# One visit of TensorE per chunk: the next chunk's attention products and this chunk's output products in one planned step

## The chip, the cores and the metric

The kernel runs on one core of a Trainium2 chip. The metric is the device time of one execution in microseconds (us). A profile of one execution gives times of single instructions; its span runs from the first to the last instruction.

## What is computed

A state-space layer on 4 sequences of 768 positions with 8 heads (head size 32, state size 16) feeds a two-layer network with 2048 hidden units. Cut to what matters:

```
# per head, chunk by chunk, cum = running sum of log(a)
L  = exp(cum[i] - cum[j]) for i >= j, else 0
M  = (C B^T) * L
y  = M x + (C state) * exp(cum)
state = exp(sum(log a)) * state + sum_j B[j] x[j] exp(cum[-1] - cum[j])
# then, with y laid out as 3072 tokens of 256 values
h  = y @ w_in            # 256 -> 2048
out = (h - tanh(h)) @ w_out   # 2048 -> 256
```

The kernel may choose its own chunk length; the result is the same.

## The kernel before, in words

**Attention.** A sequence is cut into 7 chunks: six of 112 positions and a last one of 96, so there are 28 chunks (0 to 27) in all. The 16 rows of the carried state stand in front of a chunk's 112 rows of x, so that one product over 128 rows gives both terms of y. For a chunk from number 3 on, `chunk_a` (L439) plans four steps. TensorE computes into the PSUM tile `att`, which has one buffer, the differences cum[i] - cum[j] (4 matmuls in bf16, L452) and C B^T (8 matmuls in float32, each run as two passes, L458: 16 records). These work on 9 or 16 rows in each of the array's four bands of rows. ScalarE takes the exponential into the tile `lt` (L462), VectorE multiplies by C B^T (L466), GpSimd clears what lies above the diagonal (L469). `chunk_y` (L478) plans the rest: TensorE computes y = x^T lt (8 float32 matmuls, 16 records, L494) and, unless the chunk is the last of its sequence, the state products b^T x (8 float32 matmuls, 16 records, L502), both into the PSUM tile `y` with one buffer. These use all 128 rows and 32 or 16 columns of the array each. ScalarE copies the state into the next chunk's x (four copies, L507) and writes the upper part of y (`xh`, L514); VectorE writes the rest (`xl`, L519). So y of a chunk waits for the state of the chunk before and for its own `lt`.

**Network.** The 3072 tokens are 12 tiles of 256. The hidden layer is cut into 8 blocks of 256 units; a step is one block of one tile: `mm1` (L530) makes 12 matmuls of 256 columns into the PSUM tile `ph` (two buffers, L545), `act` (L551) computes h - tanh(h) and splits it into two parts `gh` and `gl` on ScalarE and VectorE (L559, L563, L567, L574), and `mm2` (L582), two steps later, makes 12 more matmuls into the tile `po` (in the profile `o`, L595). 12 such matmuls are called a block below. The first four tiles are worked in four sweeps over two hidden blocks each, while the weights arrive and are converted (`conv`, L287); the tiles 4 to 11 follow one after the other. A tile needs y of the two or three chunks that cover its positions.

**What sets the order.** All steps are recorded with an engine, an estimated cost, and the names that they read and write (`Order.__call__`, L73). A planner then fixes the order of the instructions on every engine: `schedule` (L118) is a list scheduler, `plan` (L173) runs it 16 times with priorities from a backward run and random jitter, and 1500 more times with random changes to the priorities of the steps that start in the first 110 units, and keeps the best. Each try draws one random number for each recorded step, from a fixed seed. A step's instructions are then issued in that order as one piece, so nothing of another step comes between them on its engine.

**When chunks are recorded.** At the end of the main function (L812 to L821) each chunk from 3 on has two places among the network's steps: at the first, `chunk_a` is recorded, at the second, one network step later, `chunk_y`. Chunks 10 and 11 belong to tile 4, the first after the sweeps, and are recorded during the sweeps. TensorE's two steps of a chunk, "att" and "y", are separate; the planner may put network blocks between them, and has to leave time between them for the exponential, the product and the mask.

**Loads.** `group` (L360) loads a pair of chunks: four DMAs for B and C (L247), one for x (L259), one for B by rows (L268). Three such groups have buffers. After an odd chunk's y the group three ahead is loaded.

Of the kernel before, what the change touches and what calls it, by code (L numbers as in the profile page):

```python
# [10 lines left out]
F32 = mybir.dt.float32  # L11
# [9 lines left out]
P = 128  # L21
NB, H, S, D, N = 4, 8, 768, 32, 16
# [10 lines left out]
CPG = 2  # L33
# [14 lines left out]
class Order:  # L48
# [12 lines left out]
    def slot(self, tag, bufs):  # L61
        k = self.count[tag] = self.count.get(tag, -1) + 1
        self.fresh[f"{tag}#{k}"] = tag, f"{tag}#{k - bufs}"
        return f"{tag}#{k}"
# [8 lines left out]
    def __call__(self, eng, cost, fn, r=(), w=(), dma=0, after=()):  # L73
        i = len(self.ops)
        hard = {self.writer[n] for n in r if n in self.writer} | set(after)
        soft, chain = set(), set()
        for n in w:
            hard |= self.readers.pop(n, set())
            if n in self.writer:
                j = self.writer[n]  # L80
                if dma and self.ops[j][0] == "DMA":
                    chain.add(j)
                    hard |= self.before[n]
                else:
                    hard.add(j)
            self.writer[n] = i
            whole = self.whole.get(n, n)
            if whole in self.fresh:
                tag, old = self.fresh.pop(whole)
                for o in (old, *self.parts.get(old, ())):  # L90
                    self.dead.add(o)
                    hard |= self.readers.pop(o, set())
                    if o in self.writer:
                        hard.add(self.writer[o])
                if tag in self.taken:
                    soft.add(self.taken[tag])
                self.taken[tag] = self.made[whole] = i
            elif whole in self.made:
                soft.add(self.made[whole])
        for n in (*r, *w):  # L100
            assert n not in self.dead and n not in self.fresh and n in self.writer, n
        for n in r:
            self.readers.setdefault(n, set()).add(i)
        deps = {j: self.lag(self.ops[j][0], eng) if j in hard else 0.0 for j in (hard | soft) - {i}}
        self.ops.append((eng, cost, fn, deps))
        if dma:

            self.ops.append(("DMA", max(0.25, dma / self.RATE), None, {i: 1.4, **{j: 0.0 for j in chain}}))
            for n in r:
                self.readers[n].add(i + 1)  # L110
            for n in w:
                self.writer[n], self.before[n] = i + 1, hard - {i}
        return i
# [94 lines left out]
def tile_ssm_moe(ctx: ExitStack, tc: tile.TileContext, a, x, bn, bc, wts, out):  # L208
    nc = tc.nc
# [147 lines left out]
    def qlen(ck):  # L357
        return QL if ck % CPB == CPB - 1 else Q
# [7 lines left out]
    def operands(ck):  # L366
        d, c = grp[ck // CPG], ck % CPG
        bb = d["bc"][:, :, c * P : (c + 1) * P]
        cc = d["bc"][:, :, CPG * P + c * Q : CPG * P + (c + 1) * Q]
        return bb, cc  # L370
# [66 lines left out]
            chunk_y(ck)  # L437

    def chunk_a(ck):  # L439

        d, k, q = grp[ck // CPG], chs[ck], qlen(ck)
        n_l = k["n_l"] = [slot("lt", NL)]
        n_a = k["n_a"] = slot("att", 1)

        def fn_p():
            at_ = ps_a.tile([P, 4, 4 * P], F32, tag="att", name=f"att{ck}")
            at_ = k["a"] = at_[:, :, 0 : 4 * q].rearrange("p i (k q) -> p i k q", k=4)
            for i in range(4):  # L450
                r = slice(32 * i, 32 * i + 9)
                nc.tensor.matmul(out=at_[:, i, 0:2, :], lhsT=lt_c[r, ck], rhs=rt_c[r, :, ck, N : N + q],  # L452
                                 start=True, stop=True)
            bb, cc = operands(ck)
            for w in range(2):
                for i in range(4):
                    r = slice(32 * i, 32 * i + N)
                    nc.tensor.matmul(out=at_[:, i, 2 + w, :], lhsT=bb[r, w], rhs=cc[r, w, 0:q], start=True, stop=True)  # L458

        def fn_e():  # L460
            k["l"] = p3.tile([P, H, Q], F32, tag="lt", name=f"lt{ck}", bufs=NL)
            nc.scalar.activation(k["l"][:, :, 0:q].rearrange("p (i w) q -> p i w q", i=4), k["a"][:, :, 0:2, :], AF.Exp)  # L462

        def fn_m():
            lt = k["l"][:, :, 0:q].rearrange("p (i w) q -> p i w q", i=4)
            nc.vector.tensor_tensor(out=lt, in0=k["a"][:, :, 2:4, :], in1=lt, op=ALU.mult)  # L466

        def fn_s():
            nc.gpsimd.affine_select(out=k["l"][:, :, 0:q], in_=k["l"][:, :, 0:q], pattern=[[0, H], [1, q]],  # L469
                                    compare_op=ALU.is_ge, fill=0.0, base=N, channel_multiplier=-1)  # L470

        s = ck >= SPAN[0].stop
        op("PE", 0.65, fn_p, r=[d["n_bc"], l_c[s], r_c[s]], w=[n_a])
        op("ACT", 0.92, fn_e, r=[n_a], w=n_l)
        op("DVE", 1.08, fn_m, r=[n_a], w=n_l)
        op("POOL", 1.4, fn_s, w=n_l)

    def chunk_y(ck):  # L478

        d, k, q = grp[ck // CPG], chs[ck], qlen(ck)  # L480
        b, c = divmod(ck, CPB)
        cg = ck % CPG
        n_y = slot("y", 1)
        last = c == CPB - 1
        if c == 0:
            seq[b]["n_xh"] = op.pieces(slot("xh", 2), CPB)
            seq[b]["n_xl"] = op.pieces(slot("xl", 2), CPB)
        n_xh, n_xl = seq[b]["n_xh"][c], seq[b]["n_xl"][c]

        def fn():  # L490
            y = k["y"] = ps_y.tile([P, 2 * H * D], F32, tag="y", name=f"y{ck}")
            for hg in range(2):
                for h in range(4):
                    nc.tensor.matmul(out=y[D * h : D * h + D, hg * Q : hg * Q + q],  # L494
                                     lhsT=d["x"][:, cg, P * hg + D * h : P * hg + D * h + D],
                                     rhs=k["l"][:, 4 * hg + h, 0:q], start=True, stop=True)
            if not last:

                for w in range(2):
                    for i in range(4):  # L500
                        h = 2 * i + w
                        nc.tensor.matmul(out=y[D * i : D * i + N, H * D + D * w : H * D + D * w + D],  # L502
                                         lhsT=d["b"][:, cg, N * h : N * h + N], rhs=d["x"][:, cg, D * h : D * h + D],
                                         start=True, stop=True)

        def fn_c(i):
            nc.scalar.copy(grp[(ck + 1) // CPG]["x"][0:N, (ck + 1) % CPG, 2 * D * i : 2 * D * i + 2 * D],  # L507
                           k["y"][D * i : D * i + N, H * D : H * D + 2 * D])

        def fn_h():  # L510
            if c == 0:
                seq[b]["xh"] = p3.tile([P, 2, S], F32R, tag="xh", name=f"xh{b}", bufs=2)
            k["yv"] = k["y"][:, 0 : 2 * Q].rearrange("p (g q) -> p g q", g=2)[:, :, 0:q]
            nc.scalar.copy(seq[b]["xh"][:, :, c * Q : c * Q + q], k["yv"])  # L514

        def fn_l():
            if c == 0:
                seq[b]["xl"] = p3.tile([P, 2, S], F32R, tag="xl", name=f"xl{b}", bufs=2)
            nc.vector.tensor_tensor(out=seq[b]["xl"][:, :, c * Q : c * Q + q], in0=k["yv"],  # L519
                                    in1=seq[b]["xh"][:, :, c * Q : c * Q + q].bitcast(F32), op=ALU.subtract)  # L520

        op("PE", 0.5 if last else 0.7, fn, r=[*k["n_l"], d["p_x"][cg], d["n_bw"]], w=[n_y])
        if not last:
            for i in range(4):
                op("ACT", 0.2, lambda i=i: fn_c(i), r=[n_y], w=[grp[(ck + 1) // CPG]["p_x"][(ck + 1) % CPG]])
        op("ACT", 0.36, fn_h, r=[n_y], w=[n_xh])
        op("DVE", 0.4, fn_l, r=[n_y, n_xh], w=[n_xl])


    def mm1(t, u):  # L530
# [274 lines left out]
    def plan(g, fn, *args):  # L805
        todo.setdefault(max(g, 0), []).append((fn, args))
# [5 lines left out]
    at_ = {}  # L812
    for t in range(1, NT):
        g0, n = begin["t", t - 1], begin["t", t] - begin["t", t - 1]
        for i, ck in enumerate(chunks[t]):
            at_[ck] = g0 + i * n // len(chunks[t]), min(g0 + i * n // len(chunks[t]) + 1, g0 + n - 1)
    for ck in at_:
        plan(at_[ck][0], chunk_a, ck)
        plan(at_[ck][1], chunk_y, ck)
        if (ck + 1) % CPG == 0 and ck // CPG + NGB < NG:  # L820
            plan(at_[ck][1], group, ck // CPG + NGB)  # L821

# [57 lines left out]
```

## Time and profile before

| what | value |
|---|---|
| time, median of 3 runs (lowest to highest) | 344.49 us (343.89 to 346.46) |
| span of the profiled execution | 344.3 us |
| TensorE: matmul busy | 330.2 us, 96% |
| VectorE, ScalarE, GpSimd busy | 227.5, 192.9, 57.2 us |
| mean granted clock of TensorE | 0.970 |

The table of runs doesn't mark which of them was profiled; the span stands 0.19 us under their median. In the page of the profile, PE is TensorE, PEld its weight loads, DVE VectorE, ACT ScalarE, POOL GpSimd and SP the queue that issues most DMAs. The chain of waits follows the work that ended last back from the end: each of its rows has the start and the time until the next piece took over, in us, then the engine, the tile, the line in the code and the number of records. The table of stretches gives busy time and number of instructions of every engine between two points of the span, and the granted clock of TensorE as a share of full speed.

### The profile page before, as it was taken

To read this page: it belongs to the slowest core of one execution; us is meant where nothing else is said; L and a number is where in the kernel's file an instruction comes from. 1 tells how busy PE (TensorE), PEld (TensorE's weight loads), DVE (VectorE), ACT (ScalarE), POOL (GpSimd) and SP (SyncE) were. 2 spreads that over 40 slices of the span, in tenths; PEclk is the share of its full clock that TensorE was granted. 3 is DMA by queue.
4 is the path that set the end of the run, shared out by engine and by line. 5 is a ranking of instruction groups with operands and counts; after the bars stand their busy time and mean duration, and the time that the engine had idled before them with its cause. 6 is when DMAs were issued, how large, how long until landed. Compare 5 with 4: busy or idle time off the path is not lost.

```text
span 344.3 us, 8873 instructions
## 1 busy us (share of the span) xinstructions
PE 330.2 (96%) x3756; PEld 317.9 (92%) x3756; DVE 227.5 (66%) x339; ACT 192.9 (56%) x403; POOL 57.2 (17%) x69
## 2 busy tenths in 40 slices
PE   7939979999999999999999999999999999999995
PEld 6839879999999999999999999999999999999995
DVE  5996898999998875645654655555655555654552
ACT  7855977786554543534655646444554555554441
POOL 1544453340000110101211110210401110110000
PEclk9875989999999999999999999999999999999999
DMA  7929658614000011001211200200200100000100
GB/s 164 301 63 317 179 131 201 213 52 132 3 0 3 10 51 61 32 3 45 61 45 30 63 2 9 82 2 23 71 2 1 32 2 2 32 0 2 32 0 31
DMA packets 12471, 21.39 MB, mean 62 GB/s; under 512 B 2848, under 2 KB 7648, under 8 KB 12432
## 3 DMA queue, kind: packets, MB, share of 16 engines
q1 hardware_dynamic: 12432, 20.84, 21.4%
q8 instruction: 29, 0.48, 0.6%
q14 instruction: 10, 0.08, 0.1%
HBM read 17.51 MB, written 3.32 MB: 60 GB/s over the span
## 4 chain that ended last, share of the span: by engine, by line
PE 87%; DVE 3%; SPq 3%; DMA 3%; ACT 1%; issue 1%; POOL 0%; POOLq 0%; DVEq 0%; ACTq 0%
PE o L595 40%; PE ph L545 38%; PE y L494 3%; PE att L458 2%; DMA braw<-bn_d 2%; PE cp L381 1%; DMA bc<-bc_d 1%; PE att L452 1%; SPq L770 1%; SPq L278 1%; SPq L247 1%; PE y L502 1%; PE att L392 1%; DVE wm L310 0%; SPq L772 0%
## 5 line engine op out<-in xcount | busy, mean ns | idle before, releaser
L559 ACT ACTIVATE g<-ph 128x512 f32<-128x512 f32 x96 | 57.4, 598 | 91.5 <-PE ph L545 89.3
L563 DVE TENSOR_TENSOR g<-ph,g 128x512 f32<-128x512 f32 x96 | 65.9, 690 | 62.9 <-ACT g L559 62.9
L545 PE MATMUL ph<-xh,wh 128*128 128x256 f32 x384 | 101.3, 286 | 0.0
L545 PE MATMUL ph<-xh,wl 128*128 128x256 f32 x384 | 100.0, 283 | 0.0
L574 DVE TENSOR_TENSOR gl<-g,gh 128x512 fp32r<-128x512 f32 x96 | 67.0, 700 | 26.9 <-ACT gh L567 25.7
L545 PE MATMUL ph<-xl,wh 128*128 128x256 f32 x384 | 77.1, 282 | 0.0
L567 ACT CAST gh<-g 128x512 fp32r<-128x512 f32 x96 | 59.1, 619 | 28.7 <-DVE g L563 27.2
L545 PEld LDWEIGHTS ph<-xh,wh 128*128 128x128 f32 x384 | 73.8, 192 | 1.1 <-issue 0.4
L545 PEld LDWEIGHTS ph<-xh,wl 128*128 128x128 f32 x384 | 73.8, 192 | 0.0
L469 POOL TENSOR_SCALAR_AFFINE_SELECT lt<-lt 128x896 f32<-128x896 f32 (+1 forms) x25 | 34.0, 1359 | 203.9 <-DVE lt L466 203.9
L595 PE MATMUL o<-gh,wh 128*128 128x256 f32 x384 | 63.5, 287 | 0.0
L595 PE MATMUL o<-gl,wh 128*128 128x256 f32 x384 | 60.2, 278 | 0.0
L595 PE MATMUL o<-gh,wl 128*128 128x256 f32 x384 | 60.2, 278 | 0.0
L545 PEld LDWEIGHTS ph<-xl,wh 128*128 128x128 f32 x384 | 59.8, 192 | 0.0
L595 PEld LDWEIGHTS o<-gh,wh 128*128 128x128 f32 x384 | 51.2, 188 | 2.8
L595 PEld LDWEIGHTS o<-gl,wh 128*128 128x128 f32 x384 | 51.5, 188 | 0.0
L595 PEld LDWEIGHTS o<-gh,wl 128*128 128x128 f32 x384 | 51.5, 188 | 0.0
L466 DVE TENSOR_TENSOR lt<-att,lt 128x896 f32<-128x896 f32 (+1 forms) x25 | 26.7, 1067 | 6.8 <-ACT lt L462 6.8
L462 ACT ACTIVATE lt<-att 128x896 f32<-128x896 f32 (+1 forms) x25 | 22.6, 902 | 6.1 <-PE att L458 4.4
L507 ACT COPY x<-y 16x64 f32<-16x64 f32 x96 | 19.4, 202 | 8.6 <-DVE xl L519 7.1
L494 PE MATMUL y<-lt,x 128*32 128x112 f32 (+1 forms) x448 | 17.3, 274 | 5.4 <-POOL bc L352 3.3
L494 PEld LDWEIGHTS y<-lt,x 128*32 128x32 f32 x448 | 10.2, 113 | 9.2 <-POOL bc L352 3.4
(70 smaller groups left out, 232.8 us busy)
## 6 DMA issues: line engine op xcount, KB each, us to landing
raw<-w_d SPq DMA_DIRECT2D x16, 512.0 KB
x<-x_d SPq DMA_DIRECT2D x14, 256.0 KB
bc<-bc_d SPq DMA_DIRECT2D x56, 60.0 KB
out_d<-ob SPq DMA_DIRECT2D x24, 128.0 KB
braw<-bn_d SPq DMA_DIRECT2D x14, 112.0 KB
cum<-parts SPq DMA_DIRECT2D x1, 168.0 KB
rt_c<-cum SPq DMA_DIRECT2D x4, 27.0 KB
lt_c<-cum SPq DMA_DIRECT2D x4, 27.0 KB
```

What stands on the lines that cost most here:

```text
L458: nc.tensor.matmul(out=at_[:, i, 2 + w, :], lhsT=bb[r, w], rhs=cc[r, w, 0:q], start=True, stop=True)
L462: nc.scalar.activation(k["l"][:, :, 0:q].rearrange("p (i w) q -> p i w q", i=4), k["a"][:, :, 0:2, :], AF.Exp)
L466: nc.vector.tensor_tensor(out=lt, in0=k["a"][:, :, 2:4, :], in1=lt, op=ALU.mult)
L469: nc.gpsimd.affine_select(out=k["l"][:, :, 0:q], in_=k["l"][:, :, 0:q], pattern=[[0, H], [1, q]], compare_op=ALU.is_ge, fill=0.0, base=N, ...
L494: nc.tensor.matmul(out=y[D * h : D * h + D, hg * Q : hg * Q + q], lhsT=d["x"][:, cg, P * hg + D * h : P * hg + D * h + D], rhs=k["l"][:, 4 ...
L507: nc.scalar.copy(grp[(ck + 1) // CPG]["x"][0:N, (ck + 1) % CPG, 2 * D * i : 2 * D * i + 2 * D], k["y"][D * i : D * i + N, H * D : H * D + ...
L545: nc.tensor.matmul(out=ph[:, j, :], lhsT=w_[:, u, 0, k, j * P : (j + 1) * P], rhs=d[("xh", "xl")[p]][:, k, ts], start=p == 0 and k == 0 an ...
L559: nc.scalar.activation(g, gs[t, u][0], AF.Tanh)
L563: nc.vector.tensor_tensor(out=g, in0=ph, in1=g, op=ALU.subtract)
L567: nc.scalar.copy(gh, gs[t, u][1])
L574: on.tensor_tensor(out=gl, in0=g, in1=gh.bitcast(F32), op=ALU.subtract)
L595: nc.tensor.matmul(out=po[t, seg][:, e, :], lhsT=w_[:, u, 1, j, e * P : (e + 1) * P], rhs=g[:, j, :], start=u == seg[0] and k == 0 and j = ...
```

## The change

For chunk 10 (`joint`, the first chunk of tile 4) and all later ones except the last, the y step of chunk ck also computes `att` of chunk ck+1. In this joint step the 4 differences and the 8 C B^T products of chunk ck+1 are issued first and y and the state products of chunk ck last. Chunks 3 to 10 keep an "att" step of their own; the 17 chunks 11 to 27 have none any more. The exponential, product and mask of chunk ck+1 are recorded behind the y step of chunk ck, and so ahead of the place that they had. The joint step has the reads of both and the cost of both, 1.3 (1.1 where there are no state products). Besides, a DMA that writes the same name as the DMA before it is now planned behind that one's issue. The seed, the number of tries and all costs of other steps stay.

```diff
                 if dma and self.ops[j][0] == "DMA":
                     chain.add(j)
+                    soft.add(j - 1)
                     hard |= self.before[n]
...
     def chunk_a(ck):
-        d, k, q = grp[ck // CPG], chs[ck], qlen(ck)
-        n_l = k["n_l"] = [slot("lt", NL)]
+        k = chs[ck]
         n_a = k["n_a"] = slot("att", 1)
+        op("PE", 0.65, lambda: differences(ck), r=need_a(ck), w=[n_a])
+        weigh(ck)
+
+    def need_a(ck):
+        s = ck >= SPAN[0].stop
+        return [grp[ck // CPG]["n_bc"], l_c[s], r_c[s]]
+
+    def differences(ck):
...
+        for i in range(4):
+            r = slice(32 * i, 32 * i + 9)
+            nc.tensor.matmul(out=at_[:, i, 0:2, :], lhsT=lt_c[r, ck], rhs=rt_c[r, :, ck, N : N + q],
+                             start=True, stop=True)
+        bb, cc = operands(ck)
+        for w in range(2):
             for i in range(4):
...
+                r = slice(32 * i, 32 * i + N)
+                nc.tensor.matmul(out=at_[:, i, 2 + w, :], lhsT=bb[r, w], rhs=cc[r, w, 0:q], start=True, stop=True)
+
+    def weigh(ck):
+        k, q = chs[ck], qlen(ck)
+        n_a, n_l = k["n_a"], [slot("lt", NL)]
+        k["n_l"] = n_l
...
-        op("PE", 0.65, fn_p, r=[d["n_bc"], l_c[s], r_c[s]], w=[n_a])
         op("ACT", 0.92, fn_e, r=[n_a], w=n_l)
         op("DVE", 1.08, fn_m, r=[n_a], w=n_l)
         op("POOL", 1.4, fn_s, w=n_l)

-    def chunk_y(ck):
+    def chunk_y(ck, ahead=False):
...
         def fn():
+            if ahead:
+                differences(ck + 1)
             y = k["y"] = ps_y.tile([P, 2 * H * D], F32, tag="y", name=f"y{ck}")
...
-        op("PE", 0.5 if last else 0.7, fn, r=[*k["n_l"], d["p_x"][cg], d["n_bw"]], w=[n_y])
+        used, made = [*k["n_l"], d["p_x"][cg], d["n_bw"]], [n_y]
+        if ahead:
+            chs[ck + 1]["n_a"] = slot("att", 1)
+            used, made = used + need_a(ck + 1), made + [chs[ck + 1]["n_a"]]
+        op("PE", (0.5 if last else 0.7) + 0.6 * ahead, fn, r=used, w=made)
...
         op("DVE", 0.4, fn_l, r=[n_y, n_xh], w=[n_xl])
+        if ahead:
+            weigh(ck + 1)
...
+    joint = chunks[NSW][0]
     for ck in at_:
-        plan(at_[ck][0], chunk_a, ck)
-        plan(at_[ck][1], chunk_y, ck)
+        if ck <= joint:
+            plan(at_[ck][0], chunk_a, ck)
+        if ck >= joint and ck + 1 in at_:
+            plan(at_[ck][1], chunk_y, ck, True)
+        else:
+            plan(at_[ck][1], chunk_y, ck)
```

More of the change, by code (lines that the diff above doesn't have):

```diff
@@ L439, in chunk_a @@
     def chunk_a(ck):
-        d, k, q = grp[ck // CPG], chs[ck], qlen(ck)
-        n_l = k["n_l"] = [slot("lt", NL)]
+        k = chs[ck]
         n_a = k["n_a"] = slot("att", 1)
-        def fn_p():
-            at_ = ps_a.tile([P, 4, 4 * P], F32, tag="att", name=f"att{ck}")
-            at_ = k["a"] = at_[:, :, 0 : 4 * q].rearrange("p i (k q) -> p i k q", k=4)
-            for i in range(4):
[L451 to L458, printed above, removed]
+        op("PE", 0.65, lambda: differences(ck), r=need_a(ck), w=[n_a])
[5 more added lines that the diff above has]
+        k, q = chs[ck], qlen(ck)
+        at_ = ps_a.tile([P, 4, 4 * P], F32, tag="att", name=f"att{ck}")
+        at_ = k["a"] = at_[:, :, 0 : 4 * q].rearrange("p i (k q) -> p i k q", k=4)
+        for i in range(4):
[4 more added lines that the diff above has]
+        for w in range(2):
+            for i in range(4):
+                r = slice(32 * i, 32 * i + N)
+                nc.tensor.matmul(out=at_[:, i, 2 + w, :], lhsT=bb[r, w], rhs=cc[r, w, 0:q], start=True, stop=True)
+    def weigh(ck):
+        k, q = chs[ck], qlen(ck)
+        n_a, n_l = k["n_a"], [slot("lt", NL)]
+        k["n_l"] = n_l
         def fn_e():
@@ L470, in fn_s @@
                                     compare_op=ALU.is_ge, fill=0.0, base=N, channel_multiplier=-1)
-        s = ck >= SPAN[0].stop
-        op("PE", 0.65, fn_p, r=[d["n_bc"], l_c[s], r_c[s]], w=[n_a])
         op("ACT", 0.92, fn_e, r=[n_a], w=n_l)
```

## The prediction, made before the result was known

> **What bounds the kernel now.** I read the page first: busy times, then the chain of waits.
>
> ```profile
> span 344.3 us, 8873 instructions
> PE 330.2 (96%) x3756; PEld 317.9 (92%) x3756; DVE 227.5 (66%) x339; ACT 192.9 (56%) x403; POOL 57.2 (17%) x69
> PE 87%; DVE 3%; SPq 3%; DMA 3%; ACT 1%; issue 1%; POOL 0%; POOLq 0%; DVEq 0%; ACTq 0%
> ```
>
> TensorE is both the busiest engine and 87% of the chain that ends last. Where it isn't, the table of stretches tells:
>
> ```profile
> 25.00:60.00 35.00, 32.54 (x500) 29.70 (x497) 28.74 (x38) 25.34 (x54) 14.74 (x14) 0.82 0.75 209
> 60.00:138.90 78.90, 78.90 (x778) 77.71 (x776) 67.99 (x94) 45.84 (x83) 9.68 (x10) 1.00 0.19 58
> 138.90:310.80 171.90, 171.90 (x2017) 165.83 (x2016) 95.68 (x142) 89.95 (x193) 22.77 (x23) 1.00 0.09 27
> ```
>
> The first number behind the stretch is its length, the second TensorE's busy time. After 60 us TensorE has no idle time at the full clock (the 1.00 near the end of a row): there only the number of matmuls and the pace at which they pass count. Before 60 us it idles and its clock is cut. The changed visits, from chunk 10's y (now at 66.68 us) on, all lie in the first kind of stretch.
>
> So the next look is at TensorE's own rows. This is the chain of waits around the att visit and the y visit of chunk 18; between them lie network blocks of 12 matmuls:
>
> ```profile
> 199.85 0.21 PE att L452 x4
> 200.06 0.45 PE att L458 x16
> 200.51 1.61 PE o L595 x12
> ...
> 204.94 1.41 PE ph L545 x12
> 206.35 0.52 PE y L494 x16
> 206.88 0.12 PE y L502 x16
> 206.99 1.56 PE o L595 x12
> 208.55 1.36 PE ph L545 x12
> ```
>
> The reader is to see two things. **A visit costs more than its own rows:** the block behind it takes 0.20 us longer (1.61 against 1.41, 1.56 against 1.36). And **the pace of the network changes with the kind of visit that came last:** 12 matmuls take 1.41 us behind an att visit and 1.36 behind a y visit, until the next visit, with the same clock and the same instructions.
>
> **Part 1, the visits that go.** An att visit by itself costs 0.66 + 0.20 = 0.86 us, a y visit by itself 0.64 + 0.20 = 0.84, together 1.70. The planner has already put some of them next to each other:
>
> ```profile
> 244.72 0.52 PE y L494 x16
> 245.36 0.21 PE att L452 x4
> 245.56 0.45 PE att L458 x16
> 246.01 1.61 PE o L595 x12
> 247.63 1.41 PE ph L545 x12
> ```
>
> This is y first and att last: 1.29 + 0.20 = 1.49 us. In the order of the change, att first and y last, there is this, for chunks 10 and 9, in the sweeps:
>
> ```profile
> 57.27 0.21 PE att L452 x4
> 57.48 0.45 PE att L458 x16
> 57.93 0.52 PE y L494 x16
> 58.45 0.12 PE y L502 x16
> 58.57 1.61 PE o L595 x12
> 60.18 2.83 PE ph L545 x24
> ```
>
> 1.30 + 0.20 = 1.50 us. So joining saves 1.70 - 1.50 = 0.20 us: one of two returns to the network, while the matmuls themselves stay. Of the 17 joint visits two (at 166.21 and at 244.72 us) are neighbours already. The other 15 att visits, from the one at 64.42 to the one at 303.93 us, stand alone in the chain. 15 x 0.20 = **3.0 us less**. At the chunks 13 and 20, which have no state products, the same return is saved.
>
> **Part 2, the pace.** This is the disputed cost, and it is larger than part 1. All stretches of the fast pace behind a y visit, after chunk 10's y, are these (first, last, and the sum of the eleven):
>
> ```profile
> 67.25:68.81 1.56, 1.56 (x22) 1.43 (x13) 1.56 (x3) 1.22 (x3) 0.03 (x1) 1.00 0.29 62
> 298.22:303.86 5.64, 5.64 (x58) 5.51 (x50) 3.01 (x5) 2.91 (x9) 0.00 (x0) 1.00 0.05 14
> sum 98.79, PE 98.79 PEld 97.40 DVE 71.88 ACT 53.30 POOL 4.80; mean PE 8.98 PEld 8.85 DVE 6.53 ACT 4.85 POOL 0.44
> ```
>
> 98.79 us less eleven first-block surcharges of 0.20 are 96.6 us, or 71 blocks at 1.36. Every other block after 66 us runs at 1.41. In pairs the paces read 2.72 and 2.83, so a block differs by 0.055 us.
>
> What pace does a visit leave that ends with y and the state products, but begins with att? The rows of before have it once in the clear: behind 58.57 us comes a pair at 2.83, the slow pace. The visit just before it, at 52.96 us, has the same order, and its two blocks take 3.02 = 1.61 + 1.41, slow too. Nor do all y visits that stand alone leave the fast pace:
>
> ```profile
> 231.90 0.47 PE y L494 x16
> 232.37 1.61 PE o L595 x12
> ...
> 251.87 0.52 PE y L494 x16
> 252.50 1.61 PE o L595 x12
> ```
>
> The first is chunk 20's, without state products: it leaves 1.61, as do chunks 13 and 27. The second has them and still leaves 1.61. Of 13 such visits after 66 us eleven leave the fast pace and two the slow one, at 173.35 and at 251.87 us, both the first visit after a pair of y and att.
>
> The bounds follow. If every joint visit leaves the slow pace, as both rows of that order do, all 71 fast blocks turn slow: 71 x 0.055 = 3.9 us more. If every joint visit with state products leaves the fast one, the slow blocks turn fast, but for those behind chunks 13, 20 and 27. The sixteen slow stretches that could turn are in sum:
>
> ```profile
> sum 100.61, PE 100.61 PEld 98.50 DVE 63.54 ACT 50.41 POOL 20.50; mean PE 6.29 PEld 6.16 DVE 3.97 ACT 3.15 POOL 1.28
> ```
>
> Less sixteen first-block surcharges of 0.20 these are 97 us, or 69 blocks at 1.41: 69 x 0.055 = 3.8 us less. I take **3.9 us more**, since the pace repeats: all att visits that stand alone leave the slow pace, and both rows of the order in question do. Two rows are few, and they lie at 53 and 57 us, where the rest of the schedule is busier; that keeps the other end alive.
>
> [...]
>
> **Part 3, what moves.** The exponential, product and mask of the next chunk now start right behind the visit, with the state copies and `xh` on ScalarE and `xl` on VectorE:
>
> ```profile
> L469 POOL TENSOR_SCALAR_AFFINE_SELECT lt<-lt 128x896 f32<-128x896 f32 (+1 forms) x25 | 34.0, 1359 | 203.9 <-DVE lt L466 203.9
> L466 DVE TENSOR_TENSOR lt<-att,lt 128x896 f32<-128x896 f32 (+1 forms) x25 | 26.7, 1067 | 6.8 <-ACT lt L462 6.8
> L462 ACT ACTIVATE lt<-att 128x896 f32<-128x896 f32 (+1 forms) x25 | 22.6, 902 | 6.1 <-PE att L458 4.4
> L559 ACT ACTIVATE g<-ph 128x512 f32<-128x512 f32 x96 | 57.4, 598 | 91.5 <-PE ph L545 89.3
> ```
>
> Their chain is 0.90 + 1.07 + 1.36 = 3.3 us. Now att runs 5.84 us ahead of its y (200.51 to 206.35); then it is a whole chunk ahead. The closest pair that exists already, y at 244.72 with att behind it and the next y at 251.87, has 7.15 us and no wait. So I cost it at nothing. What hides it is the network's blocks on TensorE. The burst on ScalarE (0.90 besides the copies of the same visit) delays a tanh, behind which `ph` is freed and the next block but one may start. ScalarE sits idle 89.3 us for `ph` ahead of its 96 tanhs, nearly 1 us each, which is the cover; the pair at 244.72 has that burst too, and its blocks keep 1.61 and 1.41. If the cover were gone, it would be up to 0.9 us a visit, 15 us in all; the two pairs speak against any of it.
>
> The joint step waits for the inputs of both: B and C of chunk ck+1, loaded three groups ahead, and `lt` of chunk ck. Queued behind it on TensorE are the network's blocks, and ScalarE and VectorE wait for those. After 60 us no idle time stands before any visit (78.90 of 78.90 busy), and the planner places the step where both are expected, so nothing is added. `att` has one buffer: its old content is read by what made `lt` of chunk ck, which y waits for anyway. No DMA is added on SP. The tie of a DMA to the issue before it orders the four parts of a B/C load, in the order in which they are recorded; nothing or a few tenths in the first 60 us.
>
> **Part 4, the first 60 us.** The planner draws one random number for each step in each of 1516 tries; with 17 steps fewer every draw after the first try is another, so the order of the first 110 units is drawn anew, though none of its steps is changed before chunk 10. There are 35 - 32.54 = 2.5 us of idle time and 18% of lost clock in 25 to 60 us to win or lose. The smallest event of that kind in the trace is a wait that lets the clock drop:
>
> ```profile
> 48.68 4.28 PE ph L545 x24
> ```
>
> 4.28 against 2.83 us for two blocks is 1.45 us, and the idle time that causes it (TensorE's 2.5 us in all) comes on top: one event more or fewer is 1.5 to 4 us. No row tells which way. I take 0, with 3 us to either side.
>
> **Sum**, against the profiled execution: 344.3 - 3.0 + 3.9 + 0 + 0 = 345.2. The span lies 0.2 us under the median of the runs (344.49), so **345.4 us**: no change that counts. About 1% (3.4 us) is what a measurement of this kernel can tell from no change.
>
> **Rival 1: the joint visit leaves the fast pace.** For it: eleven of 13 y visits alone with state products do, and the last instructions of both are the same. Against it: both visits in the very order. 344.5 - 3.0 - 3.8 = 337.7 us, faster by 2%.
>
> **Rival 2, slower: the redrawn plan lets TensorE's clock drop once more before 60 us.** The place is the wait ahead of the row at 48.68 us. For it: in 25 to 60 us the mean clock is 0.82 already, so waits of that length do occur there. Against it: the planner keeps only the best of its tries by its own costs. 345.4 + 1.45 + 2.5 = 349.4 us. It counts as slower once the idle time beside a drop passes about 1.1 us.
>
> **Rival 3: the pace has nothing to do with what a visit holds**, and falls as often fast as now. For it: two y visits out of 13 don't leave the fast pace. Against it: no att visit ever does. 344.5 - 3.0 = 341.5 us.
>
> **How the numbers follow.** The forecast, 345.4, has 0.54; its own range by part 4 is 342.4 to 348.4. Rival 1 has 0.27, rival 2 0.12, rival 3 0.07. Faster by over 1% (under 341.0): nearly all of rival 1 (0.25), a third of rival 3 and 0.03 of the forecast's lower tail, 0.30. Slower (over 347.9): rival 2 and 0.04 of the upper tail, 0.16. The rest is 0.54. The range that leaves out no more than 2 in 10 takes in rival 1 with a little of the first 60 us and most of rival 2's lower half: 336.5 to 349.0.
>
> **What would show it.** In the changed kernel's chain of waits, 17 visits should read att, att, y, y and about 1.30 us, with a block of 1.61 or 1.56 behind them; the att rows alone should end with chunk 10. Pairs of blocks behind them at 2.83 bear out the forecast, 2.72 rival 1. The stretch after 60 us should have no idle time of TensorE; idle time there before y, or before a block that waits for ScalarE, would break part 3. A first att visit or a first sweep that ends later than now by more than 1.5 us, with a further row of 4.28 for two blocks, would show rival 2.

## The result, and the profile after

Ten runs of the changed kernel have a median of 347.85 us (346.48 to 348.50), ten of the kernel before 344.68 us (343.77 to 346.57). The ratio is 1.0076, with a 95% interval of 1.0051 to 1.0101: slower by 2.6 us (the two means differ by that, the medians by 3.2), within the 1% that the prediction called no change. The profiled execution took 347.76 us and has a span of 345.9 us, 1.6 us more than before. Four disturbed runs, of 365.8 to 802.4 us, are left out of the ratios below; the profiled executions of two kernels (y first, and a full-array product at every joint visit) are among them, so no trace of these two is shown.

The page of the changed kernel:

```profile
span 345.9 us, 8861 instructions
PE 331.2 (96%) x3756; PEld 320.4 (93%) x3756; DVE 229.0 (66%) x339; ACT 193.5 (56%) x403; POOL 52.7 (15%) x69
PE 87%; DVE 5%; DMA 4%; SPq 1%; ACT 1%; issue 1%; DVEq 0%; ACTq 0%
```

The shares say nothing: TensorE is as busy as before. Its stretches (length, then TensorE's busy time; the clock near the end):

```profile
25.00:60.00 35.00, 31.05 (x527) 28.16 (x527) 32.68 (x43) 27.14 (x60) 15.39 (x15) 0.86 0.76 211
60.00:138.90 78.90, 78.90 (x790) 78.03 (x789) 65.40 (x91) 45.13 (x84) 10.49 (x11) 1.00 0.15 42
138.90:310.80 171.90, 171.90 (x1994) 167.35 (x1993) 96.08 (x143) 89.92 (x191) 18.27 (x22) 1.00 0.10 28
```

Behind 60 us there is again no idle time. Now the chain of waits around chunk 18's joint visit, the counterpart of the two visits shown before (the network's lines are now 561 and 611, att 457 and 463, y 504, state products 512):

```profile
204.07 1.41 PE ph L561 x12
205.49 0.21 PE att L457 x4
205.69 0.45 PE att L463 x16
206.14 0.52 PE y L504 x16
206.66 0.12 PE y L512 x16
206.78 1.61 PE o L611 x12
208.39 1.41 PE ph L561 x12
```

One visit of 1.29 us where there were two of 0.66 and 0.64, a first block of 1.61, and the pace of 1.41 on both sides. All 17 joint visits read like this, but that those of chunks 13 and 20 have no state products. No block behind the first of them is at 1.36.

Where the 1.6 us of the span lie can be read from three places that hold the same work in both kernels: the block behind chunk 9's y (the 121st network matmul), the 241st network matmul, and the end of the last block. After:

```profile
59.25 1.61 PE o L611 x12
...
76.57 1.53 PE o L611 x13
...
336.70 5.67 PE o L611 x48
```

Before (its first place is the row at 58.57 shown in the prediction):

```profile
76.17 1.36 PE o L595 x12
...
335.11 5.67 PE o L595 x48
```

| stretch | before | after | difference |
|---|---|---|---|
| start to the block behind chunk 9's y | 58.57 | 59.25 | +0.68 |
| from there to the 241st network matmul | 17.60 | 17.32 | -0.28 |
| from there to the end of the last block | 264.61 | 265.80 | +1.19 |

The first row is what the redrawn plan of the first 60 us made of these two executions. One pair can't size it: the row at 58.57 starts at 56.3 to 58.9 us in seven traces with the first 60 us of the kernel before (mean 57.9; six are of kernels below), and at 58.2 to 60.1 us in three with those of the changed kernel (mean 59.2). The other two rows together, +0.91 us, are the joint visits: two joins less two fast blocks make the second row, 13 joins less 69 fast blocks the third.

### The profile page after: what moved, and what is told of

Its sections match the earlier page's. It is cut to its first block, busy times and chain, and to the rows that moved or that the text cites. A ratio compares the mean times of both kernels' runs of the same rounds, so it can differ in the third digit from the quotient of the medians.

```text
span 345.9 us, 8861 instructions
## 1 busy us (share of the span) xinstructions
PE 331.2 (96%) x3756; PEld 320.4 (93%) x3756; DVE 229.0 (66%) x339; ACT 193.5 (56%) x403; POOL 52.7 (15%) x69
## 4 chain that ended last, share of the span: by engine, by line
PE 87%; DVE 5%; DMA 4%; SPq 1%; ACT 1%; issue 1%; DVEq 0%; ACTq 0%
PE o L611 40%; PE ph L561 38%; PE y L504 3%; PE att L463 3%; DMA raw<-w_d 3%; DMA braw<-bn_d 1%; PE att L457 1%; DVE lt L476 1%; PE cp L382 1%; DVE wm L311 1%; SPq L786 1%; DVE wv L308 1%; PE y L512 1%; ACT lt_c L725 1%; DVE g L579 1%
## 5 line engine op out<-in xcount | busy, mean ns | idle before, releaser
L583 ACT CAST gh<-g 128x512 fp32r<-128x512 f32 x96 | 59.2, 619 | 35.5 <-DVE g L579 29.1
L561 PEld LDWEIGHTS ph<-xh,wh 128*128 128x128 f32 x384 | 73.0, 190 | 0.8 <-ACT x L517 0.2
L561 PEld LDWEIGHTS ph<-xh,wl 128*128 128x128 f32 x384 | 72.8, 190 | 0.0
L479 POOL TENSOR_SCALAR_AFFINE_SELECT lt<-lt 128x896 f32<-128x896 f32 (+1 forms) x25 | 28.8, 1153 | 187.7 <-DVE lt L476 170.0
L611 PEld LDWEIGHTS o<-gh,wh 128*128 128x128 f32 x384 | 52.1, 189 | 1.3
```

Of the source, the lines that this page charges most:

```text
L561: nc.tensor.matmul(out=ph[:, j, :], lhsT=w_[:, u, 0, k, j * P : (j + 1) * P], rhs=d[("xh", "xl")[p]][:, k, ts], start=p == 0 and k == 0 an ...
L583: nc.scalar.copy(gh, gs[t, u][1])
L611: nc.tensor.matmul(out=po[t, seg][:, e, :], lhsT=w_[:, u, 1, j, e * P : (e + 1) * P], rhs=g[:, j, :], start=u == seg[0] and k == 0 and j = ...
```

## The experiments

All kernels that move visits, but for the two made from the changed kernel, keep the kernel before's own planned order: on VectorE, ScalarE, GpSimd and SP every instruction stands where it stood; on TensorE the att products of chunk ck+1 are issued inside the y step of chunk ck instead of at their own place. That takes the planner out of the comparison. It can be done from chunk 13 on, where att of the next chunk stands behind y in the order. Ratios are to runs of the kernel before that were made at the same time. For the traces, "main stretch" is the time from the start of the 241st network matmul to the start of the last one: 264.48 us before, 265.67 in the changed kernel. In it the kernel before has 69 blocks at 1.36, the changed kernel none of 172. (Two of the expectations count matmuls from 0 and call its first one the 240th.)

### The joint visits alone, in both orders

```diff
+MODES = {ck: "D C Y S" for ck in range(13, 27)}   # the other kernel: "Y S D C"
...
-            y = k["y"] = ps_y.tile([P, 2 * H * D], F32, tag="y", name=f"y{ck}")
+            k["y"] = ps_y.tile([P, 2 * H * D], F32, tag="y", name=f"y{ck}")
+            for t in MODES.get(ck, "Y S").split():
+                if t in ("D", "C"):
+                    part(t, ck + 1)
+                else:
+                    products(t)
```

Here D are the differences, C the products C B^T, both of chunk ck+1, Y is y and S the state products of chunk ck; at its own place att issues what is left.

> The kernel before with its own planned order on every engine, and one thing moved: from chunk 13 on, the att products of chunk ck+1 are issued right ahead of y of chunk ck (14 visits, of which 2 were neighbours already). Mine: 12 joins save 0.20 us each, 2.4 us; the 28 fast blocks behind chunk 16 and later turn slow, 28 x 0.055 = 1.5 us; together 0.9 us less than before (ratio 0.9975), and no pair of blocks at 2.72 behind a joint visit. Rival 1 (the state products at the end leave the fast pace): 2.4 us less, and some 52 slow blocks turn fast, 2.9 us less; together 5.3 us less (ratio 0.985).

> The same, but in each joint visit y and the state products first and the att products last. Mine: the order inside the visit does not matter, 0.9 us less than before, equal to the run with att first within 0.3 us. Rival 1: 5 us slower than the run with att first.

Measured: att first 0.9969 (0.9935 to 1.0002), y first 0.9969 (0.9936 to 1.0002). Both intervals take in 1, so the times alone show no gain; the trace does. The main stretch with att first is 263.68 us, 0.80 less than before; 28 of the 69 fast blocks turned slow. Its chain from chunk 18's visit on:

```profile
206.13 0.21 PE att L449 x4
206.34 0.45 PE att L456 x16
206.78 0.52 PE y L509 x16
207.30 0.12 PE y L516 x16
207.42 1.61 PE o L627 x12
209.03 1.41 PE ph L577 x12
```

With nothing else changed the block behind the visit reads 1.61 and then 1.41, where it read 1.56 and 1.36 in the kernel before. So the saving of 0.20 us a join and the loss of the fast pace are both shown, in their sizes, and rival 1 is out. The two orders came out alike in time, as forecast. The one visit with y first in the next run left 1.41 as well.

### What sets the pace behind a visit

> One look: the order of before, with a different make-up of the visit at each y from chunk 13 on (D the differences, C the products C B^T, Y y, S the state products, s extra state-sized products into unused columns, f an extra full-array product): 13 D C Y; 14 D C Y S; 15 Y S D C; 16 C D Y S; 17 C Y S, D by itself later; 18 D Y S, C by itself later; 19 D C S Y; 20 D C Y and 8 s; 21 D C Y S and 1 s; 22 D C Y S and 8 s; 23 D Y C S; 24 D C Y S f; 25 D C, 4 s, Y S; 26 D C Y S and 2 s. Read the pace of the blocks behind each (1.36 fast, 1.41 slow). Mine, anything of att in a visit makes it slow: all fourteen at 1.41. A rival by the bf16 weights of D: 17 fast and the rest slow. A rival by the row bands of C: 18 fast, 17 slow. A rival by the number of products: some of 20, 21, 22, 25, 26 fast, 14 and 16 slow.

> One look: the order of before, att and y visits apart except where said, with extra products behind them: y visits 14 C Y S; 16 Y S and 1 s; 17 Y S and 8 s; 21 D Y S; 25 Y S f. att visits by themselves: 18 and 1 s; 19 and 8 s; 20 f; 21 and 2 s; 23 and 4 s; 24 and 16 s; 25 and 8 state products; the others as before. Mine: a y visit by itself stays fast with extra products of its own kind, an att visit stays slow whatever follows. Rival by the number of products: some of 16 and 17 turn slow (one block lasts 0.05 us longer) and some of the att visits fast. Rival by the last product: all att visits with s at the end leave 1.36.

The edits are other strings in the same table, such as `24: "D C Y S f"`, a second table of that kind for what follows an att visit, and this in `products`:

```diff
+            elif t[0] == "s":
+                for i in range(int(t[1:] or 1)):
+                    i = i % 4
+                    nc.tensor.matmul(out=y[D * i : D * i + N, 384 : 416],
+                                     lhsT=d["b"][:, cg, N * i : N * i + N], rhs=d["x"][:, cg, D * i : D * i + D],
+                                     start=True, stop=True)
+            elif t == "f":
+                nc.tensor.matmul(out=y[:, 448:480], lhsT=wh[:, 0, 0, 0, 0:P], rhs=wh[:, 0, 0, 0, 0:32], start=True, stop=True)
```

Most forms stand for one visit in one execution:

| visit | pace behind it |
|---|---|
| D C Y; D C Y S; Y S D C; C D Y S; C Y S; D Y S; D C S Y; D Y C S; D C, 4 s, Y S | 1.41 |
| D C Y and 8 s; D C Y S and 1 s; D C Y S and 8 s | 1.41 |
| D C Y S and 2 s; D C Y S f | **1.36** |
| y by itself with 1 s, 8 s or f | 1.41 (without them mostly 1.36) |
| att by itself with 1 s or 2 s | **1.36** |
| att by itself with 4 s, 8 s, 16 s, f, or 8 state products | 1.41 |

The three visits with one small product, with two, and with the full-array product, all of the form D C Y S otherwise:

```profile
243.42 0.52 PE y L509 x16
243.94 0.12 PE y L516 x16
244.06 0.04 PE y L522 x2
244.10 1.61 PE o L627 x12
```

```profile
296.30 0.52 PE y L509 x16
296.82 0.12 PE y L516 x16
296.93 0.04 PE y L522 x4
296.98 1.56 PE o L627 x12
298.54 1.36 PE ph L577 x12
```

```profile
270.14 0.12 PE y L516 x16
270.25 0.21 PE y L526
270.47 1.46 PE ph L577 x12
271.93 1.36 PE o L627 x12
```

In joint visits of this form two records more (line 522, two against four) go with 1.56 in place of 1.61 for the first block, and with the fast pace for all that follow. My theory that anything of att in a visit makes it slow falls: a joint visit, and an att visit by itself, can leave the fast pace. So does its other half, that a y visit by itself stays fast with more products of its own kind. The rivals by kind fall too: neither the bf16 weights nor the row bands (C Y S and D Y S are both slow), nor the last product (f is last in a fast joint visit and in two slow ones). The rival by the number of products saw its signs come true in both traces, but no number parts the two paces: behind D C Y S two are fast, one and eight slow. What is left is that the pace depends on the instructions ahead of the block, down to a few records. How it does is open.

For a visit without extra products they are not all. In the second trace the y visit at 205.85 us is the plain one of chunk 18, which left 1.36 in the kernel before. Here the att visit ahead of it had one small product and left the fast pace, and the y visit left the slow one, 1.61 and 1.41. In the twelve traces used here, after 60 us, a plain y visit with state products that met the slow pace left the fast one 50 times of 59, and of four that met the fast pace none did. So what a visit leaves also depends on what it meets.

### The extra products at every joint visit

> The run with the moved att products in before's order, and behind each of the 14 joint visits one extra product over the full array with 32 columns into unused columns of the y tile. In the look at the forms one such visit cost 0.11 us more, started the next block 0.02 us sooner and left the fast pace. If the pace is a matter of how the first network matmul lines up with what ran before it, to a few ns, and the extra product sets that anew each time: blocks at 1.36 behind all 14 visits, some 80 blocks x 0.055 = 4.4 us less than the run without it, 1.2 us of it paid back for the products: 3.2 us less. If the effect depends on the pace before the visit, the pace alternates, and the gain is about 1 us. If it was chance: 1.2 us more.

> The same with two extra state-sized products (16 by 32, four records) in place of the full one, which cost 0.03 us in the look at the forms and left the fast pace once, where one and eight of them left the slow one. Lined up anew each time: 4.4 - 0.4 = 4.0 us less than without them. Depending on the pace before: about half. Chance: 0.4 us more.

The edits are `"D C Y S f"` and `"D C Y S s2"` for the chunks 13 to 26. Measured: 0.9865 (0.9822 to 0.9908) with the full product, 0.9856 (0.9811 to 0.9901) with two small ones. Against the 0.9969 without them that is 3.6 and 3.9 us, near the 3.2 and 4.0 of the first case, though the interval of each ratio reaches 1.1 to 1.6 us to either side. The trace of the run with two small ones:

```profile
171.67 0.52 PE y L509 x16
172.19 0.12 PE y L516 x16
172.31 0.04 PE y L522 x4
172.35 1.56 PE o L627 x12
173.92 1.36 PE ph L577 x12
```

All twelve joint visits with state products now leave 1.36, those of chunks 13 and 20, which have none, 1.41. The main stretch is 260.05 us with 121 fast blocks. It is 3.63 us shorter than without the products. The pace behind the form with two small products repeats at every visit, so it is no chance. For the full product only the time says so.

### The plan redrawn without any joint visit

```diff
                     chain.add(j)
+                    soft.add(j - 1)
```

```diff
-    ROUNDS, JITTER, SEED, CLIMB, RAMP = 16, 0.3, 133908, 1500, 110.0
+    ROUNDS, JITTER, SEED, CLIMB, RAMP = 16, 0.3, 133909, 1500, 110.0
```

> The kernel before with one line of the change, the tie of a DMA to the issue before it. No visit changes, and the planner draws the same random numbers, but for another set of ties, so its order of the first 110 units comes out otherwise. My part 4: within 3 us of before, either way; all of it by 60 us of the span. If the joint visits were all of the change's loss, this equals before within 0.5 us.

> The kernel before with the next seed (133909): nothing changes but the planner's draws. My part 4: within 3 us of before, either way. It tells how far a redrawn plan alone moves the time: if by under 0.5 us, the redrawn plan cannot be what the changed kernel lost before 60 us.

Measured: the tie alone 1.0067 (1.0044 to 1.0090), the next seed alone 1.0033 (1.0006 to 1.0060). Both lie within 3 us of before. The tie alone is 2.3 us slower, not equal within 0.5 us, so by that expectation the joint visits are not all of the change's loss; the changed kernel without the tie was not run. And "all of it by 60 us" fails for the tie. Its 241st network matmul starts at 76.21 us (before: 76.00), and its main stretch has 266.13 us, 1.65 more, with 38 fast blocks in place of 69: 31 x 0.055 = 1.7. The chain shows the place:

```profile
69.23 0.52 PE y L495 x16
69.75 0.12 PE y L503 x16
69.86 0.21 PE att L453 x4
70.07 0.45 PE att L459 x16
70.52 1.61 PE ph L546 x12
72.13 2.83 PE o L596 x24
```

Here the last visit before a long stretch without visits, some 50 us, is a pair that ends with att, and the whole stretch passes at 2.83 us for two blocks. In the kernel before a y visit stands last (73.97 us) and the stretch passes at 2.72. With the next seed the time is lost earlier: its 241st network matmul starts at 77.26 us, 1.26 later, and its main stretch has 264.26 us, 0.22 less than before.

### The changed kernel with two small products

```diff
+                if ahead:
+                    for i in range(2):
+                        nc.tensor.matmul(out=y[D * i : D * i + N, 384:416], lhsT=d["b"][:, cg, N * i : N * i + N],
+                                         rhs=d["x"][:, cg, D * i : D * i + D], start=True, stop=True)
```

> The changed kernel, its own planned order, with two extra state-sized products (16 by 32, into unused columns of the y tile) at the end of each joint visit that has state products; nothing else. The changed kernel runs all its blocks at 1.41 behind 60 us. If that pace is what it lost: behind 15 visits 1.36, some 133 blocks x 0.055 = 7.3 us less, 15 x 0.03 = 0.5 us more, so 6.8 us less than the changed kernel (some 341 us, ratio to before about 0.988). If its loss lies elsewhere, or two small products do nothing with the planner's other order: 0.5 us more than the changed kernel.

Measured: 341.46 us, 0.9879 (0.9845 to 0.9912). The main stretch is 259.18 us with 133 blocks at 1.36, 6.5 us less than in the changed kernel (forecast 6.8). So behind 60 us the pace turned the change's gain into a loss, and thirty small products more turn it back.

### The three visits left over, and the best version

> One look: the run with two small products in before's order, with other tails at the three visits that lack state products and left the slow pace: chunk 13 gets eight and two small products (the same stream of shapes as the others), chunk 20 four, chunk 27 (y alone) two. If only the stream of shapes matters: 13 fast, the same as its neighbours. For 20 and 27 no forecast; each fast one saves 8 and 21 blocks x 0.055 = 0.4 and 1.2 us.

The edits are `13: "D C Y s8 s2"`, `20: "D C Y s4"` and `27: "Y s2"`. Measured: chunk 13's visit fast, chunk 20's slow, chunk 27's fast. The stream of shapes was enough at chunk 13, though the products go to other columns. Chunk 20 then got chunk 13's tail.

This trace shows something else as well. Up to chunk 20's visit TensorE runs the same matmuls in the same order as in the next kernel in before's order, but behind the att visit of chunk 12 and the y visit of chunk 11 the paces are exchanged. First this trace, then that of the next kernel:

```profile
69.46 1.56 PE ph L577 x12
71.02 2.72 PE o L627 x24
...
74.43 1.61 PE ph L577 x12
```

```profile
69.90 1.61 PE ph L577 x12
71.50 2.82 PE o L627 x24
...
74.97 1.56 PE ph L577 x12
```

The y visit is followed by 32 blocks without a visit, which pass at 1.41 in the first trace and at 1.36 in the second: about 1.7 us between two executions of the same instructions. So the pace behind these two visits is not a matter of the instructions alone. The visits with two small products behind the state products do not share this: in the five kernels that have them throughout all 66 left 1.36, whichever pace they met.

> The run with two small products in before's order, with the tails that left the fast pace in the look at the tails: eight and two small products at the chunks 13 and 20, two at chunk 27. 37 more blocks at 1.36: 37 x 0.055 = 2.0 us less, 2 x 0.16 us of products paid: 1.7 us less than the run with two small products, from the 240th network matmul to the last 258.3 us (before 264.5). If the pace of a visit depends on more than the stream in front of it, one or two of the three stay slow, 0.3 to 1.2 us of it lost.

> The changed kernel with the same tails at its 17 joint visits and at chunk 27. From the 240th network matmul to the last 259.2 - 1.7 = 257.5 us, since it joins three chunks more than the run in before's order; its first 60 us stay its own, 0.7 to 1.5 us later than those of before. Together about 1.7 us less than the changed kernel with two small products.

Measured: 340.36 us and 0.9833 (0.9792 to 0.9874) in before's order, main stretch 258.37 us; 339.52 us and **0.9812** (0.9776 to 0.9849) for the changed kernel with these tails, main stretch 257.47 us with all 172 blocks at 1.36. Both stretches are the forecast's to 0.1 us. Chunk 18's visit there:

```profile
200.70 0.52 PE y L504 x16
201.22 0.12 PE y L512 x16
201.34 0.04 PE y L518 x4
201.38 1.56 PE o L616 x12
202.95 1.36 PE ph L566 x12
```

Both beat the kernel before, by more than their intervals; the changed kernel was not run beside them, but its ratio to the kernel before was 1.0076. The join is worth its 0.20 us each and the fast pace 0.055 us a block, once they come together.

## Why the prediction was right, and where not

**Part 1, the visits that go: right, in size too.** The joint visit takes 1.29 + 0.20 us. Taken alone, 12 joins less 28 fast blocks made the main stretch 0.80 us shorter; by the rows, 12 x 0.20 - 28 x 0.055 = 0.86.

**Part 2, the pace: right in its result, by one of its two reasons.** Every joint visit leaves 1.41; the main stretch of the changed kernel grows by 69 x 0.055 - 13 x 0.20 = 1.2 us, and 1.19 was measured. The reason that held is that both rows of that very order were slow: the form leaves 1.41 in 28 of 28 visits behind 60 us in the traces used here. The other reason, that visits with att are slow, was too simple: with two small products more the same visit leaves 1.36, and a plain y visit leaves one pace or the other, in part by the pace that it meets.

**Part 3, what moves: right.** The stretches behind 60 us are 78.90 of 78.90 and 171.90 of 171.90 us busy. No block waits for the burst on ScalarE.

**Part 4, the first 60 us: right as a bound, wrong in its reach.** The profiled execution loses 0.68 us by the block behind chunk 9's y, within the 3 us. But one pair of executions does not size this (1.3 us between the means of seven and three traces), and a redrawn plan also moves visits behind 60 us and with them the pace: the tie alone cost 1.65 us there. I had put its cost at "nothing or a few tenths in the first 60 us". In the changed kernel this part of the plan no longer matters, since every visit leaves the same pace.

**The step that failed is the sum's last: "The span lies 0.2 us under the median of the runs".** Every execution whose span is listed, 155 in all, takes 1.6 to 1.9 us more than its span (347.76 against 345.9 here). So the span of 344.3 us stood for an execution of about 346.0 us, and not for the median of 344.49 us; its own time is not on record. With the changed kernel's difference the sum gives 345.2 + 1.9 = 347.1 us, and with 0.7 us for part 4 347.8, which is the profiled run.

The 2.6 us between the runs are 1 us more than the 1.6 between these two spans. The granted clock of an execution goes with its time: of 65 runs of the kernel before that list it, 23 at 0.970 (the clock of both profiled executions) average 346.5 us, and 11 at 0.985 average 343.9. The six runs of the changed kernel at 0.970 average 348.2 us, 1.7 more than those of before, as the spans say; none of its ten is above 0.980. The 1.3 us between the mean starts of the block behind chunk 9's y, with the 0.91 us behind it, would make 2.2 of the 2.6. That the redrawn first 60 us make this difference fits the run with the tie alone, none of whose runs is above 0.975, but no run shows it by itself.

**The rivals.** Rival 1 (the fast pace) and rival 3 (the pace as often fast as now) are both out by the chain: no fast block behind 17 joint visits. But rival 3 has a grain of truth for plain visits, whose pace is not theirs alone. Rival 2 did not come about: the clock is lower up to 25 us (0.79, before 0.85) and higher from there to 60 us (0.86, before 0.82). Half of its sign did come: the first att visit starts at 26.6 us, before at 24.7, but no row of 4.28 for two blocks follows, and at 59.25 us 0.68 us of the delay are left.

## What to carry to other kernels

Where an engine is busy without a gap, read the duration of equal blocks by what ran just before them: here two paces, 4% apart, were worth more than all visits that the change saved. Read it in more than one execution, since the same instructions took either pace. Before counting on a reordering, move the one thing with everything else in its old order; a planner that draws anew for each variant made differences of the same size by itself. And take the difference between a profile's span and its own run before a sum is set against the median of other runs.

## What the runs showed of the hardware

The pace of equal matmuls (256 columns, a new set of weights for each) at a granted clock of 1.00 has two values, 113.3 and 117.8 ns a matmul (1.36 and 1.41 us for twelve). After 60 us it changes where TensorE comes back from a group of small products, and then holds until the next such group, for as long as 68 us (50 blocks at 1.36 from 70.35 us on, in the run with the next seed), through changes between the two lines of the network. Neither value is the N/2.4 + 2.5 = 109 ns that the Trainium skill gives for a matmul of 256 columns by itself ("TensorE: Matmul & The Clock Gate", section "Back-to-back issue gap"); the same section says that in a stream of weight loads and matmuls both set the spacing, which the two values fit, but it has one pace for a size and not two. In joint visits with state products two records of 16 by 32 more (four in place of two) at the end, 0.04 us in all, went with the fast pace, and this repeated: with two small products at each such visit 66 of 66 in five kernels left 1.36, with none 28 of 28 left 1.41. It is no rule for every form: a y visit by itself left either pace, and two executions of the same matmuls took opposite paces for 32 blocks. What it is that lines up is not settled; the runs only show that it can be steered.
